# One transfer of weights at the end of a decode step comes as eight

## The chip, the cores and the metric

The kernel runs on one core of one Trainium2 chip. A core has a matrix engine (PE, with its weight loads shown apart as PEld), a vector engine (DVE), a scalar engine (ACT), a general engine (POOL) and SP, which here only issues transfers; 16 DMA engines move the data between the chip's memory (HBM) and the on-chip buffer of 128 partitions. The metric is the device time of one execution in microseconds (us). The kernel before took 527.71 us, the median of three runs from 527.6 to 528.53.

## The reference

Two equal layers work on one token of 640 numbers. Each is attention over a window of 4096 cached keys and values (32 heads of 192), and then a gated feed-forward network of 1536 columns, both with a layer norm in front and a residual sum behind. In short:

```
x = x + A(layernorm(x), k_cache, v_cache, wq, wo)
x = x + B(layernorm(x), w1, w3, w2)
x = x + A(layernorm(x), k_cache, v_cache, wq, wo)
x = x + B(layernorm(x), w1, w3, w2)

def B(x, w1, w3, w2):
    gate = x @ w1          # 640 -> 1536
    up = x @ w3            # 640 -> 1536
    h = silu(gate) * up
    return h @ w2          # 1536 -> 640
```

All weights and caches are bf16, and both layers use the same ones. With one token every weight is used once a layer, so the work is little beside the bytes: 221 MB are read.

## The kernel before

All large operands pass through one buffer, the arena, of 16 slots of 128 partitions by 6144 bf16 (12 KB a partition). A list, `loads`, written out ahead, holds every transfer in the order in which it is to be issued: for each layer wq, then keys and values head by head, then wo, then w1, w3 and w2. `refill()` takes entries from the front of that list as long as slots are free, and issues each of their parts as one transfer from SP (line 243). `done()` frees a slot when its last reader has been written out, and calls `refill()` again. SP does nothing else but issue these, and, at the very end, the transfer of the output (line 531). `pin()` keeps the order of the program on each engine.

The framework gives each transfer a completion semaphore; in the trace eight of them are handed out in turn (numbers 100, 102 and 105 to 110). A transfer's completion is marked by its DMA engines on that semaphore.

In layer 1 the feed-forward part has its weights in these entries: `("fa", 1)`, all of w1, 1920 KB in one transfer; `("fb", 1)`, the first four fifths of w3, 1536 KB; `("fc", 1)`, the rest of w3, 384 KB; and `("fd", 1)`, the first 5760 columns of w2 as it lies on the partitions (nine of its twelve chunks of 640 columns), in three transfers of 3840, 1280 and 640 columns, 960, 320 and 160 KB. The last three chunks of w2 stay in the tile `keep` since layer 0. The third transfer of `("fd", 1)` is the last load of the whole kernel.

`ffn(1)` multiplies by w1, turns the result and forms the gate, multiplies by w3, forms h in `htd`, and calls `last_rows`. That goes through the twelve chunks of w2 in the order 9, 10, 11 (from `keep`), 0 to 8 (from the arena); each is four small matmuls (tile `pss`, line 80, where the helper `mm` records all matmuls) that sum into one place. Chunks 0 to 5 lie in the first of the three transfers, 6 and 7 in the second, 8 in the third. Then DVE casts the sum (line 529) and SP sends it out (line 531). After that only the waits that close the program follow (line 603).

Where a matmul reads what several transfers have written, it stands behind all of them. All 128 partitions of a chunk are summed in one matmul, so a chunk is needed whole.

Of the kernel before, what the change touches and what calls it, by code (L numbers as in the profile page):

```python
# [15 lines left out]
P = 128  # L16
# [9 lines left out]
PGW = 6144  # L26
# [21 lines left out]
def kernel(  # L48
# [13 lines left out]
    nc = tc.nc  # L62
# [12 lines left out]
    def pin(ins):  # L75
        tc.keep_in_program_order(ins)
        return ins
# [61 lines left out]
    arena = arn.tile([P, NSLOT * PGW], BF16, name="arena")  # L139
# [6 lines left out]
    loads = []  # L146
# [5 lines left out]
    w2_v = B_w2.rearrange("(p f) n -> p (f n)", f=12)  # L152
# [3 lines left out]
    def slots(key, width):  # L156
        return [key] + [key + (i,) for i in range(1, -(-width // PGW))]

    def head(layer, g):
        return HG * ORDER[layer][g // HG] + g % HG  # L160

    def k_head(layer, g):
        return HG * ORDER[1][0] + (0, 3, 1, 2, 6, 4, 5, 7)[g] if layer == 1 and g < HG else head(layer, g)

    def k_first(layer, i):
        return layer == 0 and H - HB <= i < H
# [6 lines left out]
    def wo_units(layer):  # L173
        order = wo_order(layer)
        ends = (0, 8, 17, 26, 35, 44, 48) if layer == 0 else (0, 12, 24, 36, 44, 48)
        return [order[a:b] for a, b in zip(ends, ends[1:])]

    for layer in range(2):
        for c0, c1 in ((0, 1), (1, 2), (2, 3), (3, 5)) if layer == 0 else [(c, c + 1) for c in range(NCH)]:
            w = PGW // 2 if layer == 1 and c1 == NCH else PGW * (c1 - c0)  # L180
            loads.append(([("q", layer, c) for c in range(c0, c1)],
                          [(o, w, wq_r[:, PGW * c0 + o:PGW * c0 + o + w]) for o in range(0, PGW * (c1 - c0), w)]))
        for i in range(H + LEAD):
            kinds = (("v", i - LEAD, A_v_cache), ("k", i, A_k_cache))
            for kind, g, cache in kinds[::-1] if k_first(layer, i) else kinds:
                if not 0 <= g < H:
                    continue
                h = k_head(layer, g) if kind == "k" else head(layer, g)
                if kind == "k" and layer == 1 and h in RETAIN:
                    if h == STASH:  # L190
                        loads.append(([("k", 1, h)], []))
                    continue
                loads.append(([(kind, layer, h)],
                              [(0, PGW, cache[0, h, S0:SK, :].rearrange("(p t) d -> p (t d)", p=P))]))
        units = wo_units(layer)
        for w, unit in enumerate(units):
            parts = []
            for at, ci in enumerate(unit):
                blk, e = ORDER[layer][ci // 12], ci % 12
                if parts and parts[-1][2] == blk and parts[-1][3] + parts[-1][1] == e:  # L200
                    parts[-1][1] += 1
                else:
                    parts.append([at, 1, blk, e])
            if layer == 1 and w + 2 == len(units):
                (at, n, blk, e), = parts
                parts = [[at, n - 3, blk, e], [at + n - 3, 3, blk, e + n - 3]]
            parts = [(640 * at, 640 * n, wo_v[blk][:, 640 * e:640 * (e + n)]) for at, n, blk, e in parts]
            if w + 1 < len(units):
                loads.append((slots(("o", layer, w), 640 * len(unit)), parts))
            elif layer == 0:  # L210
                assert len(parts) == 1 and parts[0][1] == 2560
                loads.append((None, [(wo5[:], parts[0][2])]))
        rows = 4 if layer == 0 else 5
        loads.append((slots(("fa", layer), 1536 * rows), [(0, 1536 * rows, w1_v[:, 0:1536 * rows])]))
        loads.append(([("fb", layer)], [(0, PGW, w3_v[:, 0:PGW])]))
        if layer == 0:
            loads.append(([("fc", layer)], [(0, 1536, w1_v[:, PGW:]), (1536, 1536, w3_v[:, PGW:]),
                                            (3072, 2560, w2_v[:, 0:2560])]))
            loads.append(([("fd", layer)], [(0, 3200, w2_v[:, 2560:5760])]))
            loads.append((None, [(keep[:], w2_v[:, 5760:7680])]))  # L220
        else:
            loads.append(([("fc", layer)], [(0, 1536, w3_v[:, PGW:])]))
            loads.append(([("fd", layer)], [(o, n, w2_v[:, o:o + n]) for o, n in ((0, 3840), (3840, 1280), (5120, 640))]))

    def refill():
        while loads:
            keys, parts = loads[0]
            if keys is None:
                for dst, src in parts:
                    pin(nc.sync.dma_start(out=dst, in_=src))  # L230
                loads.pop(0)
                continue
            n = len(keys)
            at = [s for s in free if all(s + i in free for i in range(n))]
            if not at:
                return
            s = at[0]
            for i, key in enumerate(keys):
                free.remove(s + i)
                home[key] = s + i  # L240
            loads.pop(0)
            for off, w, src in parts:
                pin(nc.sync.dma_start(out=arena[:, s * PGW + off:s * PGW + off + w], in_=src))
            if not parts:
                stash(arena[:, s * PGW:s * PGW + PGW], False)

    def stash(x, save):
        xu, pu, ru = x.bitcast(U32), pss[:].bitcast(U32), rest[:].bitcast(U32)
        at = 0
        for t, lo, n in [(pu, 512 * k, 512) for k in range(5)] + [(pu, MB + MN, 512 - MN), (ru, 0, MN)]:  # L250
            a, p = xu[:, at:at + n], t[:, lo:lo + n]
            pin(nc.vector.tensor_copy(out=p if save else a, in_=a if save else p))
            at += n
# [4 lines left out]
    def done(*keys):  # L258
        for key in keys:
            free.append(home.pop(key))  # L260
        refill()
# [272 lines left out]
    def attention(layer):  # L534
# [36 lines left out]
        wo_proj(layer)  # L571

    refill()
    for layer in range(2):
        attention(layer)
# [32 lines left out]
```

## Time and profile before

| | us |
|---|---|
| median of three runs (527.6 to 528.53) | 527.71 |
| the profiled execution's own time | 527.9 |
| its span, first to last instruction | 526.2 |
| PE busy | 278.6 |
| DVE busy | 257.9 |
| ACT busy | 62.0 |
| POOL busy | 16.3 |
| last 160 KB of w2: issued at | 507.18 |
| its time from issue to landing | 15.7 |
| output transfer: issued at | 523.62 |

Times in the profile count from the first instruction. "Busy" is the time in which an engine ran instructions. A transfer's issue is the short instruction on SP that starts it; its landing is the moment when its last completion mark arrives. The granted TensorE clock was 0.697 of full speed in the mean over the span. Over the span 422 GB/s were moved.

### The profile page before, as it was taken

The page shows a single profiled execution, that of the slowest core. Times are in us where ns is not written, and L with a number is a line of the kernel's source. Part 1 is how long each engine was busy: PE and PEld are TensorE (multiplying, and loading weights), DVE is VectorE, ACT ScalarE, POOL GpSimd, SP SyncE. Part 2 cuts the span into 40 slices and gives each one's busy share as a digit, 9 for nine tenths or more (in the row PEclk, how much of TensorE's full clock was granted, in tenths as well). Part 3 has the DMA queues.
Part 4 walks back from the last instruction along what each step waited for, and adds up shares of the span by engine and source line. Part 5 has one row for each costly group of instructions (what it writes and reads, how often), then busy time and mean ns, then how long its engine had stood idle before and what let it go on. Part 6 is the DMA issues. An engine that isn't in the chain of part 4 may idle for free.

```text
span 526.2 us, 5967 instructions
## 1 busy us (share of the span) xinstructions
PE 278.6 (53%) x2403; PEld 114.8 (22%) x2403; DVE 257.9 (49%) x389; ACT 62.0 (12%) x192; POOL 16.3 (3%) x76
## 2 busy tenths in 40 slices
PE   3434654473655645645545566687254756355545
PEld 1111221131212211212112222233022322122122
DVE  1099875556757476653002137722476655753001
ACT  1001120110202020102001002022111120102000
POOL 4000000000000000000000000000000000001000
PEclk9657878667766776586556557988657886686558
DMA  8999999999999999999999999999999999999995
GB/s 345 432 430 429 428 428 432 430 430 429 428 430 427 428 432 431 426 430 420 418 429 424 424 429 427 430 427 431 426 430 428 430 426 432 429 429 428 433 425 240
DMA packets 21779, 221.80 MB, mean 422 GB/s; under 512 B 2552, under 2 KB 2680, under 8 KB 4856
## 3 DMA queue, kind: packets, MB, share of 16 engines
q1 hardware_dynamic: 21608, 221.42, 99.2%
q8 instruction: 19, 0.31, 0.2%
q14 instruction: 8, 0.07, 0.0%
q10 hardware_dynamic: 144, 0.00, 0.0%
HBM read 221.41 MB, written 0.00 MB: 421 GB/s over the span
## 4 chain that ended last, share of the span: by engine, by line
DMA 46%; PE 5%; DVE 4%; issue 1%; ACT 0%; SPq 0%; DVEq 0%; ACTq 0%
DMA arena<-in_A_v_cache_dram 24%; DMA arena<-in_A_wo_dram 9%; DMA arena<-in_A_k_cache_dram 7%; DMA arena<-in_B_w_dram 4%; DVE arena L330 3%; DMA arena<-in_A_wq_dram 2%; PE s_ps L80 1%; PE y_ps L80 1%; PE o_ps L80 1%; PE q_ps L80 1%; PE pss L80 1%; PE g_ps L80 0%; DVE w L278 0%; ACT w L364 0%; DVE lt L352 0%
## 5 line engine op out<-in xcount | busy, mean ns | idle before, releaser
L80 PE MATMUL s_ps<-arena,wst 128*32 128x512 bf16 x768 | 154.7, 519 | 167.1 <-DVE arena L330 84.1
L330 DVE STREAM_TRANSPOSE arena<-arena 128x1536 uint32<-128x1536 uint32 x100 | 171.1, 1754 | 61.8 <-DMA arena<-in_A_k_cache_dram 61.4
L80 PE MATMUL o_ps<-arena,ptm 128*8 128x384 bf16 (+1 forms) x1024 | 113.2, 422 | 17.6 <-DMA arena<-in_A_v_cache_dram 17.6
L80 PEld LDWEIGHTS <-wst 128*32 128x32 bf16 x768 | 53.7, 117 | 251.9 <-issue 224.5
L80 PEld LDWEIGHTS <-ptm 128*8 128x8 bf16 (+1 forms) x1030 | 40.1, 99 | 54.9 <-issue 43.6
L361 ACT ACTIVATE nt<-m 32x16 f32<-32x16 f32 x16 | 3.4, 213 | 271.5 <-DVE m L358 271.5
L377 ACT COPY ptm<-w 32x64 bf16<-32x64 bf16 x80 | 23.6, 295 | 47.8 <-PE o_ps L80 45.4
L80 PE MATMUL q_ps<-arena,xs 128*32 128x512 bf16 x120 | 17.8, 599 | 15.6 <-DMA arena<-in_A_wq_dram 13.0
L410 DVE SCALAR_TENSOR_TENSOR w<-pss,sc,cb 64x192 bf16<-64x192 f32 x16 | 6.7, 417 | 37.3 <-PE pss L80 34.2
L80 PE MATMUL y_ps<-arena,otd 128*1 128x320 bf16 x176 | 15.1, 461 | 14.3 <-DMA arena<-in_A_wo_dram 14.3
L312 POOL COPY wst<-qt_sb 32x24 bf16<-32x24 bf16 x30 | 8.4, 281 | 432.7 <-PE s_ps L80 311.9
L367 DVE STREAM_TRANSPOSE w<-w 64x512 bf16<-64x512 bf16 x16 | 11.3, 705 | 14.4 <-ACT w L364 14.4
L352 DVE TENSOR_REDUCE lt<-s_ps 64x1 f32<-64x512 f32 x16 | 11.0, 684 | 14.0 <-PE s_ps L80 13.7
L377 DVE COPY ptm<-w 32x64 bf16<-32x64 bf16 x48 | 9.9, 207 | 15.7 <-PE o_ps L80 14.7
L278 DVE CAST w<-y_ps 128x320 bf16<-128x320 f32 x3 | 1.5, 492 | 32.9 <-PE y_ps L80 32.9
L80 PEld LDWEIGHTS <-xs 128*32 128x32 bf16 x200 | 8.8, 117 | 33.9 <-issue 25.2
L297 DVE CAST w<-q_ps 128x256 bf16<-128x256 f32 x2 | 0.8, 424 | 31.1 <-ACT w L296 31.1
L382 DVE RECIPROCAL sc<-pss 64x1 f32<-64x1 f32 x16 | 2.6, 166 | 21.5 <-PE pss L80 21.4
L403 ACT CAST w<-o_ps 128x384 bf16<-128x384 f32 x16 | 7.7, 478 | 35.3 <-PE o_ps L80 26.3
L80 PEld LDWEIGHTS <-otd 128*1 128x1 bf16 x192 | 6.5, 107 | 23.7 <-issue 19.5
L364 ACT ACTIVATE w<-s_ps,nt 64x512 bf16<-64x512 f32 x16 | 10.9, 682 | 5.7 <-DVE nt L362 5.7
L80 PE MATMUL pss<-w,sel 128*64 128x192 bf16 x32 | 6.5, 293 | 7.9 <-ACT w L403 5.1
(78 smaller groups left out, 111.2 us busy)
## 6 DMA issues: line engine op xcount, KB each, us to landing
arena<-in_A_v_cache_dram SPq DMA_DIRECT2D x64, 1536.0 KB, 29.2
arena<-in_A_k_cache_dram SPq DMA_DIRECT2D x50, 1536.0 KB, 29.2
arena<-in_A_wq_dram SPq DMA_DIRECT2D x7, 1536.0 KB, 9.3
arena<-in_A_wo_dram SPq DMA_DIRECT2D x3, 1920.0 KB, 31.6
arena<-in_B_w_dram SPq DMA_DIRECT2D x3, 1536.0 KB, 11.5
arena<-in_A_wq_dram SPq DMA_DIRECT2D x1, 3072.0 KB, 19.5
arena<-in_A_wo_dram SPq DMA_DIRECT2D x2, 1440.0 KB, 8.6
arena<-in_A_wo_dram SPq DMA_DIRECT2D x2, 960.0 KB, 8.1
```

The lines of the kernel that those rows point to most:

```text
L80: return pin(nc.tensor.matmul(*a, **k))
L278: pin(nc.vector.tensor_copy(out=y_sb[:, 320:640], in_=y_ps[1][:, 0:320]))
L312: pin((engs[a].copy if engs[a] is nc.scalar else engs[a].tensor_copy)(out=dst, in_=src))
L330: pin(nc.vector.transpose(x[:, w * sp:w * (sp + 1)].bitcast(U32), x[:, w * sp:w * (sp + 1)].bitcast(U32)))
L352: pin(nc.vector.reduce_max(out=t0[:, 0:1], in_=s_ps[0:64, :], axis=AX.X))
L361: pin(nc.scalar.mul(out=tb[32:64, :].rearrange("p (a z) -> p a z", a=4)[:, :, 0:HB], in_=mb, mul=-SCALE))
L364: pin(nc.scalar.activation(out=e[:], in_=s_ps[0:64, :], func=ACTF.Exp, bias=nbt[:, 0:1], scale=SCALE, accum_out=l[0:64]))
L367: pin(nc.vector.transpose(et[:], e[:]))
L377: pin((eng.copy if eng is nc.scalar else eng.tensor_copy)(out=dst, in_=src))
L382: pin(nc.vector.reciprocal(out=rl[half], in_=rl_ps[half]))
L403: pin(nc.scalar.copy(out=o_sb[:, 0:384], in_=o_ps[:, 0:384]))
L410: pin(nc.vector.scalar_tensor_tensor(out=om, in0=ot_ps[half], scalar=rl[half], in1=mask[half].unsqueeze(2).broadcast_to([64, 16, 12]), op0 ...
```

## The change

The last transfer, chunk 8 of w2 for layer 1 (640 columns, 1280 bytes on each of 128 partitions), is replaced by eight transfers of the same columns that take 64, 14, 12, 10, 8, 6, 4 and 10 of the partitions, in this order. To this end a part in `loads` may carry a first partition and a number of partitions, and `refill()` uses them. What is computed, and all other transfers and their order, stay as they are.

```
-            loads.append(([("fd", layer)], [(o, n, w2_v[:, o:o + n]) for o, n in ((0, 3840), (3840, 1280), (5120, 640))]))
+            parts = [(o, n, w2_v[:, o:o + n]) for o, n in ((0, 3840), (3840, 1280))]
+            p0 = 0
+            for rows in (64, 14, 12, 10, 8, 6, 4, 10):
+                parts.append((5120, 640, w2_v[p0:p0 + rows, 5120:5760], p0, rows))
+                p0 += rows
+            assert p0 == P
+            loads.append(([("fd", layer)], parts))
...
-            for off, w, src in parts:
-                pin(nc.sync.dma_start(out=arena[:, s * PGW + off:s * PGW + off + w], in_=src))
+            for off, w, src, *rows in parts:
+                p0, n = rows or (0, P)
+                pin(nc.sync.dma_start(out=arena[p0:p0 + n, s * PGW + off:s * PGW + off + w], in_=src))
```

## The prediction

> **What bounds the kernel now.** I read the page's 40 slices first: the DMA row stands at 9 from the second slice to the last but one, so the loads set the pace and the arithmetic hides behind them. The change touches only the last 160 KB, so the rest is read from the chain that ended last, whose tail is:
>
> ```profile
> 474.66 32.51 DMA arena<-in_A_wo_dram
> 507.16 0.02 issue
> 507.18 15.71 DMA arena<-in_B_w_dram
> 522.90 0.04 issue
> 522.94 0.27 PE pss L80 x4
> ```
>
> Columns are start, length and what. The load that is to be cut up is issued at 507.18 and lands at 522.90; the four matmuls of the last chunk start 0.04 later, then one cast (0.32) and the output transfer. Every us by which the landing moves, the end moves. The chain also goes back from the issue at 507.18 to the landing of *another* load, 0.02 earlier. Counting the issues of SP, that load (474.66) is the eighth before it. So I looked at what SP waits for between 486 and 510 us:
>
> ```profile
> SPq L243 <- DMA arena<-in_A_wo_dram: 12.6, 3, 4.2
> SPq L243 <- DMA arena<-in_A_v_cache_dram: 10.5, 3, 4.0
> ```
>
> All six last issues of line 243 waited for a landing. The semaphores of the trace say which: loads take eight completion semaphores in turn, and each issue waits until the earlier load of its own semaphore has landed. Even the output transfer, next in SP's order, passes such a wait at 509.1, before it waits for its data:
>
> ```profile
> L531 SPq EVENT_SEMAPHORE  x1: 14502/14502/14502, 509.1 to 509.1; - x1
> ```
>
> So never more than eight loads are under way, and a load's issue time is the landing time of its eighth predecessor. From the page's issue rows (KB, median us from issue to landing) these landings follow:
>
> ```profile
> arena<-in_B_w_dram SPq DMA_DIRECT2D x1, 960.0 KB, 23.6
> ...
> arena<-in_B_w_dram SPq DMA_DIRECT2D x1, 320.0 KB, 19.9
> arena<-in_B_w_dram SPq DMA_DIRECT2D x1, 160.0 KB, 15.7
> ```
>
> The 960 KB load, issued at 498.10, lands at 521.7; the 320 KB one, issued at 502.63, at 522.5. The last view is the DMA share stage by stage (us; PE, PEld, DVE, ACT, POOL busy; clock; DMA share; GB/s):
>
> ```profile
> 518.00:519.00 1.00, 0.50 (x10) 0.35 (x14) 0.55 (x3) 0.00 (x0) 0.00 (x0) 0.84 1.02 419
> 519.00:520.00 1.00, 1.00 (x18) 0.39 (x8) 0.00 (x0) 0.00 (x0) 0.00 (x0) 1.00 0.77 314
> 520.00:521.00 1.00, 0.40 (x4) 0.00 (x0) 0.55 (x1) 0.00 (x0) 0.00 (x0) 1.00 0.57 224
> 521.00:522.00 1.00, 0.65 (x28) 0.57 (x31) 0.20 (x2) 0.00 (x0) 0.00 (x0) 1.00 0.23 90
> 522.00:523.00 1.00, 0.75 (x36) 0.43 (x24) 0.00 (x0) 0.00 (x0) 0.00 (x0) 1.00 0.14 41
> ```
>
> The engines run dry one after the other: the 16 completion marks of the last load come between 519.15 and 522.90. The slowest engine alone sets the landing.
>
> **The change part by part.** The removed transfer put 8 rows of 1280 B on each of 16 engines. On the slowest they cost 0.37 us (its mark for the 320 KB load is at 522.53, for this one at 522.90), 46 ns a row. The first new transfer, 64 rows, leaves 4 on each. If none of the seven small ones reaches the slowest engine it is done 4 x 46 = 0.18 us sooner, if all do, 3 rows or 0.14 us later. That is the whole effect on the data itself.
>
> The larger term is the issue. Eight transfers take eight semaphores, so each waits for a landing of its own. In their order these are, from issue plus time to landing and to the hundredth from the trace's semaphore marks: 507.16 (as now), 509.07 and 510.28 (two wo loads), 514.82 (the 1920 KB load of w1), 518.45 and 519.39 (w3), 521.74 (the 960 KB of w2) and 522.53 (the 320 KB). None of these moves, since the pieces stand behind them on every engine. SP needs 0.33 us for an issue, and the gaps are wider, so SP itself is no limit. The first six pieces are issued by 519.4 and are over before the end: even at the upper 2.49 us worked out below, the sixth lands at 521.9. The seventh, issued at 521.76, is always 0.8 us ahead of the eighth. The eighth, 10 rows, can't be issued before 522.55, when almost all data is in. Nobody covers what follows: the last chunk's matmuls need all 128 rows. Behind it on SP only the output transfer waits; its own semaphore is by then that of the first piece, done at about 522.7, so it adds no wait.
>
> How long does a lone small load take from issue to landing? No row before shows one on empty engines, so I bound it from the two ends of the trace, where the engines were idle:
>
> ```profile
> 1.20:1.70 0.50, 0.00 (x0) 0.00 (x0) 0.00 (x0) 0.50 (x1) 0.50 (x4) 1.00 0.00 0
> 1.70:1.80 0.10, 0.00 (x0) 0.00 (x0) 0.00 (x0) 0.10 (x1) 0.10 (x2) 1.00 3.59 614
> ...
> 523.50:524.80 1.30, 0.00 (x0) 0.00 (x0) 0.05 (x1) 0.00 (x0) 0.00 (x0) 1.00 0.00 0
> ```
>
> SP's first load is issued at 0.74 (0.39 us of issue) and its first packet starts at 1.75; the output transfer is issued at 523.62 (0.65 us) and its first packet starts at 524.87. Both come 0.60 to 0.62 us after the issue has ended. The output's four rows are marked as landed by 525.27, 1.65 us after its start. The very first 12 KB packets took 0.74 to 1.28 us where later ones took 0.46, so a first read costs 0.28 to 0.82 us more. A completion mark comes 0.10 us (deep queue) to 0.34 us (output) after its packet. The row takes 0.055. Lower end: 0.33 + 0.62 + 0.06 + 0.28 + 0.10 = 1.39 us. Upper end: 0.65 + 0.62 + 0.06 + 0.82 + 0.34 = 2.49 us. The nearest row is the output transfer, a few rows on idle engines: 1.65 + 0.28 for the read = 1.93 with its issue of 0.65, or 1.61 with the 0.33 of nearly all loads. Nothing tells the two apart, so I take the middle, 1.77.
>
> By the Trainium skill (DMA: Bandwidth & Descriptors, section on the anatomy of one DMA, given there for the GpSimd path) a transfer costs about 2.0 us whatever its size, most of it the confirmation of the write, and the page says to coalesce small transfers. With 2.0 in place of 1.77 the time would be 0.23 us longer, 529.5; the trace's 1.65 for the output lies a little under that figure.
>
> Before the last chunk's matmuls PE now waits for eight semaphores where it waited for one. A waiting instruction on PE takes 0.051 us (its rows on line 603). Those for early pieces pass beforehand; if the last piece's is asked first, up to seven follow: 0 to 0.36 us, and as SP's rows on line 603 pair two semaphores, I take two, 0.10.
>
> Sum: issue 522.55 + 1.77 = 524.32 against 522.90, +1.42, plus 0.10 gives +1.52 us. The profiled execution took 527.9 us (span 526.2), 0.19 above the median of 527.71. So 529.4 on its own scale, and 529.23, say 529.2, beside the median.
>
> **The rivals.** *No wait, a better balance.* If the eight transfers could all be queued by 520.9, so that a lone one would land by 522.7, the slowest engine would set the end with as few as 4 rows, and the end would come 0.18 us earlier: 527.5. For it: the marks spread over 3.75 us, so shifting rows off late engines is what the data needs. Against it: every one of the last issues waits on its own semaphore's landing. 10%. By the Trainium skill (same page, section on why a DMA increments its semaphore by 16) a transfer uses the largest number of engines up to 16 that divides its rows, the lowest-numbered ones; engines 14 and 15 would then keep 4 rows and engines 0 to 3 get 11. The output's 4 rows agree: 12 marks at once at 524.64, four more at 525.21 to 525.27. Which engines are late the trace doesn't say.
>
> *Pieces that wait for each other.* If pieces with the same columns counted as overlapping, each would wait for the one before to land: first landing about 522.7, seven more at 1.77 + 0.05 each, 535.4, 12.5 us later, or 540.3. Against it: copies into the same columns of ptm, other rows, run abreast on two engines:
>
> ```profile
> 243.41 1.54 ACT L377 COPY ptm<-w 32x64 bf16<-32x64 bf16 x5 [2.44 <-PE o_ps L80]
> 243.42 0.42 DVE L377 COPY ptm<-w 32x64 bf16<-32x64 bf16 x2 [1.71 <-PE o_ps L80]
> ```
>
> 4%.
>
> **How the numbers follow.** About 0.2%, 1.06 us, is what a measurement of this kernel can tell from no change. The forecast, a last piece issued at 522.55, has 85%; 1% is left for what I don't see. Its own ends: 1.39 - 0.35 + 0 = +1.04 and 2.49 - 0.35 + 0.36 = +2.50, so 528.75 to 530.2; the median itself moves by 0.1 to 0.2 between runs, which makes the range 528.5 to 530.3. It leaves out the two rivals and a little of the forecast's edges. Of the 85%, 5% ends under +1.06. Faster 0.01, same 0.10 + 0.05 = 0.15, slower 0.84 (forecast 0.80, waiting pieces 0.04).
>
> **What would show it.** In the profile after: seven more issues on SP, at about 509.1, 510.3, 514.8, 518.5, 519.4, 521.8 and 522.55; the last piece 1.4 to 2.5 us from issue to landing; the chain's end passing from the 320 KB load through SP to a short load; a DMA share near zero for about a us before the last matmuls; four matmuls 0.04 to 0.4 us behind that landing, and all after that as now. I am wrong if the eighth piece is issued before 520.9, if a lone load lands in under 1.4 us, or if issues stand 1.8 us apart.

## The result and the profile after

The changed kernel takes 529.59 us (median of eight runs), the kernel before, on the same chips, 527.91. The ratio is 1.0034 with a 95% interval of 1.0023 to 1.0044, so 1.2 to 2.3 us slower. Forecast were 529.2 us and +1.5 us. The profiled span went from 526.2 to 527.7 us; a second profile of the kernel before, taken later, has 526.0.

The end of the chain that ended last, after (start, length, what):

```profile
502.28 20.36 DMA arena<-in_B_w_dram
522.63 0.02 issue
522.65 1.41 DMA arena<-in_B_w_dram
524.06 0.35 issue
524.41 0.27 PE pss L80 x4
524.68 0.02 issue
524.70 0.32 DVE w L536
```

Where before one load ran from 507.18 to the end, the chain now goes from the 320 KB load, landed at 522.63, through SP to a piece of 10 rows that is issued 0.02 us later and takes 1.41 us. Then there are 0.35 us, which were 0.04 before, until the four matmuls. From their start to the end of the span it takes 3.3 us, as before.

SP's issues in order of time (start, length), one view for each:

```profile
506.83 0.58 SPq L250 DMA_DIRECT2D arena<-in_B_w_dram  x1
...
514.55 0.28 SPq L250 DMA_DIRECT2D arena<-in_B_w_dram  x1
518.20 0.27 SPq L250 DMA_DIRECT2D arena<-in_B_w_dram  x1
519.11 0.27 SPq L250 DMA_DIRECT2D arena<-in_B_w_dram  x1
521.87 0.25 SPq L250 DMA_DIRECT2D arena<-in_B_w_dram  x1
522.65 0.28 SPq L250 DMA_DIRECT2D arena<-in_B_w_dram  x1
```

Two more stand at 508.74 and 509.94. These are the eight forecast times within 0.4 us. The DMA share by stage around the last issue (us; PE, PEld, DVE, ACT, POOL; clock; DMA share; GB/s) shows the empty time that follows it:

```profile
522.80:523.20 0.40, 0.19 (x8) 0.00 (x0) 0.00 (x0) 0.00 (x0) 0.00 (x0) 1.00 0.01 3
523.20:523.50 0.30, 0.00 (x0) 0.00 (x0) 0.00 (x0) 0.00 (x0) 0.00 (x0) 1.00 0.00 0
523.50:523.80 0.30, 0.00 (x0) 0.00 (x0) 0.00 (x0) 0.00 (x0) 0.00 (x0) 1.00 0.14 43
```

The ten rows of the last piece move between 523.5 and 523.7; no other load moves data from 523.0 on.

One thing in the trace was not forecast. These are the latest completion marks of each load after the change, worked out from the trace's semaphore marks, with the number of rows:

```
320 KB load                      522.63
64 rows  (piece 1)               522.84
14 rows  (piece 2)               523.03
12 rows  (piece 3)               523.24
10 rows  (piece 4)               523.43
 8 rows  (piece 5)               523.63
 6 rows  (piece 6)               523.84
 4 rows  (piece 7)               523.26
10 rows  (piece 8)               524.06
```

Pieces 2 to 6 were issued by 519.1, yet their last marks come 0.19 to 0.21 us apart, one row each, where a row was worth 46 ns. A slow engine that takes part in all six of them would be done at 523.84 even if nothing had been issued late. So there were two theories for the experiments. **L** (late issue): the eighth piece waits for the 320 KB load, then needs 1.41 us, then PE 0.35. **M** (marks): every piece in which an engine takes part costs it about 0.2 us.

### The profile page after: what moved, and what is told of

It reads as the page before. It is cut to its first block, busy times and chain, and to the rows that moved or that the text cites. A ratio compares the mean times of both kernels' runs of the same rounds, so it can differ in the third digit from the quotient of the medians.

```text
span 527.7 us, 5977 instructions
## 1 busy us (share of the span) xinstructions
PE 287.6 (55%) x2403; PEld 117.7 (22%) x2403; DVE 257.9 (49%) x389; ACT 62.1 (12%) x192; POOL 16.3 (3%) x76
## 4 chain that ended last, share of the span: by engine, by line
DMA 45%; PE 6%; DVE 4%; ACT 1%; issue 1%; SPq 0%; DVEq 0%; ACTq 0%
DMA arena<-in_A_k_cache_dram 19%; DMA arena<-in_A_v_cache_dram 9%; DMA arena<-in_A_wo_dram 9%; DMA arena<-in_B_w_dram 4%; DVE arena L337 3%; PE s_ps L80 2%; DMA keep<-in_B_w_dram 2%; DMA arena<-in_A_wq_dram 2%; PE o_ps L80 1%; PE y_ps L80 1%; PE q_ps L80 1%; PE pss L80 1%; ACT w L371 0%; DVE lt L359 0%; PE g_ps L80 0%
## 5 line engine op out<-in xcount | busy, mean ns | idle before, releaser
L80 PE MATMUL s_ps<-arena,wst 128*32 128x512 bf16 x768 | 160.5, 537 | 158.6 <-DVE arena L337 79.3
L80 PE MATMUL o_ps<-arena,ptm 128*8 128x384 bf16 (+1 forms) x1024 | 115.0, 429 | 18.8 <-DMA arena<-in_A_v_cache_dram 18.8
L80 PEld LDWEIGHTS <-wst 128*32 128x32 bf16 x768 | 54.9, 120 | 246.9 <-issue 221.9
L80 PE MATMUL q_ps<-arena,xs 128*32 128x512 bf16 x120 | 18.9, 623 | 16.6 <-DMA arena<-in_A_wq_dram 14.0
```

The source lines that it names most:

```text
L80: return pin(nc.tensor.matmul(*a, **k))
```

## The experiments

Apart from the waits of PE taken early, the pieces ahead of the 320 KB load, the kernel before once more and the halves by columns, every edit is to the list of rows alone, which is `(64, 14, 12, 10, 8, 6, 4, 10)` in the changed kernel. "X" below is the latest mark of the 320 KB load in the same profile; before, the last landing was X + 0.37.

**Five pieces, all issued early**

```
-            for rows in (64, 14, 12, 10, 8, 6, 4, 10):
+            for rows in (64, 16, 16, 16, 16):
```

> Two theories of the 1.5 us. Theory L (late issue): the last piece is issued only when the 320 KB load has landed and then needs 1.41 us, and PE needs 0.35 us for eight waits. Theory M (marks): in the trace after, the marks of the first six pieces on the slowest DMA engine come 0.20 us apart (522.84, 523.03, 523.24, 523.43, 523.63, 523.84) although a row costs it 0.05, so every piece that an engine takes part in costs it about 0.2 us, however few its rows. This kernel has five pieces of 64, 16, 16, 16 and 16 rows: the same bytes on every engine as one transfer, and the last piece is issued when the 1536 KB load of w3 has landed (about 518.2), far ahead of the end. L: the last landing is as before, 0.4 us behind the last mark of the 320 KB load, and only one or two more waits on PE cost 0.1 to 0.2: 0.1 to 0.2 us slower than before. M: the slowest engine ends its 64-row share 0.21 us behind its last mark of the 320 KB load and then needs 4 x 0.2, so landing 1.0 us behind that mark: 0.7 to 0.9 us slower than before.

Measured: 1.0027 (1.0017 to 1.0038), 0.9 to 2.0 us slower. The chain's end and two stages of the DMA share:

```profile
518.11 5.38 DMA arena<-in_B_w_dram
523.49 0.09 issue
523.58 0.27 PE pss L80 x4
```

```profile
522.00:522.40 0.40, 0.34 (x20) 0.18 (x9) 0.00 (x0) 0.00 (x0) 0.00 (x0) 1.00 0.09 29
522.40:522.80 0.40, 0.25 (x8) 0.10 (x7) 0.00 (x0) 0.00 (x0) 0.00 (x0) 1.00 0.00 0
```

The last piece is issued at 518.11 and lands at 523.49, X + 0.98 (X is 522.51), as M said (1.0). The latest marks of the five pieces stand at 522.68, 522.89, 523.09, 523.29 and 523.49. All data has moved by 522.4, as the second view shows: no packet after that (the last ends at 522.38). So it isn't the rows that take 0.2 us each but the completion marks, the last of which trails the last row by 1.1 us. Without any late issue, pieces of one row for each engine make the kernel slower. The time lies above the 0.7 to 0.9 us that M gave; about 0.2 us of it comes after the output has landed, as the run with four quarters shows below.

**Eight pieces, six of them on two engines alone**

```
+            for rows in (96, 2, 2, 2, 2, 2, 2, 20):
```

> Eight pieces of 96, 2, 2, 2, 2, 2, 2 and 20 rows. If a two-row piece goes to two engines alone, the slowest engine (which took part in the six-row piece of the kernel after, but not in its four-row piece) has the first and the last piece only: two marks. The last piece is still issued when the 320 KB load has landed. L: as the kernel after, landing 1.4 us behind that load, PE 0.35 us: about 1.5 us slower than before. M alone: landing 0.5 to 0.6 us behind the 320 KB load's last mark (0.3 for six rows, 0.2 for one more piece), with PE's waits 0.3 to 0.5 us slower than before.

Measured: 1.0045 (1.003 to 1.006). The chain:

```profile
522.58 1.52 DMA arena<-in_B_w_dram
524.11 0.35 issue
524.46 0.33 PE pss L80 x4
```

The 96 rows are complete at X + 0.19 and none of the six small pieces has a mark behind 523.12, so M has nothing to say here, and still the end comes at X + 1.54: issue at 522.58, 1.52 us for the load, 0.35 for PE. L alone is enough as well, though 1.6 to 3.2 us are a little more than the 1.5 it gave.

**The waits of PE taken early**

```
         for fcx in (9, 10, 11, 0, 1, 2, 3, 4, 5, 6, 7, 8):
             pg, off = w2_chunk(1, fcx)
+            if fcx == 8:
+                mm(pss[0:1, 512:513], lhsT=htd[0:118, 8:9], rhs=pg[0:118, off:off + 1], start=True, stop=True)
```

> The kernel after with one more matmul of one column ahead of the last chunk, into an unused place, that reads rows 0 to 117 of the chunk, so that it waits for the first seven pieces; only the last piece's wait is left for the last chunk. If PE's 0.35 us between the last landing and the matmuls are the eight waits in a row, this falls to 0.05 to 0.1 and the time is 0.25 to 0.3 us under the kernel after (1.2 to 1.3 us slower than before). If the 0.35 us are something else (PE gone cold, the landing seen late), it stays at 0.35 and the time is that of the kernel after. The landing itself stays 1.4 us behind the 320 KB load.

Measured: 1.0029 (1.0018 to 1.004), span 527.4 against 527.7. The chain:

```profile
521.83 1.53 DMA arena<-in_B_w_dram
523.36 0.51 issue
523.87 0.16 PE pss L80
524.03 0.03 issue
524.06 0.27 PE pss L80 x4
```

The load in the first line is piece 7, with 4 rows. The last piece lands at 524.02 and the four matmuls start at 524.06: 0.35 us became 0.04, and 0.51 us of waits now stand ahead of the extra matmul, beside the last piece's way. In the time alone the gain can't be told, as the interval overlaps that of the changed kernel (1.0023 to 1.0044). In the changed kernel these waits are three instructions in PE's queue, the first of which asks for the last piece's semaphore together with that of piece 7; the others, though long satisfied, follow it at 0.1 us each. The view names the group without the semaphores, which stand in the trace:

```profile
L80 PEldq EVENT_SEMAPHORE  x3: 51/51/51, 524.1 to 524.3; - x3
```

**Seven pieces, the last issued 0.76 us earlier**

```
+            for rows in (64, 14, 12, 10, 8, 6, 14):
```

> Seven pieces of 64, 14, 12, 10, 8, 6 and 14 rows: the last is issued when the 960 KB load has landed (0.76 us earlier than in the kernel after). L alone: it lands 1.4 us after that, 0.65 us behind the last mark of the 320 KB load, PE 0.25 to 0.35: 0.5 to 0.7 us slower than before. M: the slowest engine, in all seven pieces, still ends at 0.21 + 6 x 0.2 = 1.41 us behind that mark, so as the kernel after, 1.4 to 1.6 us slower than before: the two causes end together in the kernel after and taking one away gives nothing.

Measured: 1.0036 (1.0023 to 1.0049), as the changed kernel: nothing that can be measured was won by issuing earlier. In its profile the slowest engine's marks go 522.69, 522.89, 523.08, 523.28, 523.48, 523.68 and 523.89, which is X + 1.40, where M put it, although the last piece was issued at 521.75. One further row landed only at 525.26 in that execution: a 16 KB instruction fetch occupied a DMA engine from 522.7 for 1.5 us, and a row's packet starts as it ends (that both ran on one engine is read from these times alone). That mishap is part of neither theory; the profiled execution took 530.88 us, where the median of its kernel is 529.07.

**Two halves and four quarters by rows**

```
+            for rows in (64, 64):
```

> Two pieces of 64 rows, both issued far ahead of the end. In the run with five pieces the marks of one engine came 0.17 to 0.20 us apart although all rows had been moved 1.1 us before the last mark, so the theory M is now: two marks of one engine are never under 0.17 to 0.20 us apart. Four rows take 0.18 us by themselves, so each of the two marks comes when its data allows it: landing 0.37 to 0.42 us behind the last mark of the 320 KB load, as before, and one more wait on PE: within 0.1 us of before. If a piece had a fixed cost on top of its rows instead (0.15 us and 0.05 a row), two pieces would land 0.7 us behind that mark: 0.3 to 0.4 us slower than before.

```
+            for rows in (32, 32, 32, 32):
```

> Four pieces of 32 rows, two rows on every engine in each, the last one issued when the 1920 KB load has landed, far ahead of the end. M: four marks 0.20 apart, landing 0.8 us behind the last mark of the 320 KB load instead of 0.37: 0.4 to 0.5 us slower than before, with PE's waits up to 0.6. Rows alone (46 ns each): landing as before, 0 to 0.2 us slower through PE's waits. A fixed cost on top of the rows: 4 x (0.15 + 0.1) = 1.0 us, 0.6 to 0.8 us slower.

Measured: two halves 1.0013 (1.0004 to 1.0022), four quarters 1.0019 (1.001 to 1.0028). The chains, first of the halves, then of the quarters:

```profile
522.77 0.04 issue
522.82 0.31 PE pss L80 x8
523.12 0.04 issue
523.16 0.27 PE pss L80 x4
```

```profile
514.77 8.71 DMA arena<-in_B_w_dram
523.48 0.04 issue
523.52 0.27 PE pss L80 x4
```

The halves land at X + 0.35 (marks 0.18 and 0.17 apart) and the quarters at X + 0.62 (0.16, 0.15, 0.15, 0.16). So a mark has no cost on top of its rows; two marks of one engine simply came no closer than 0.15 to 0.2 us in these profiles. That gives M its form: four rows hide it, two rows do so in part, one row doesn't. But the landings, -0.02 and +0.25 us against X + 0.37, don't explain the ratios, 0.7 and 1.0 us in the middle. X itself is later, 522.77 and 522.86. And the end of the program is longer: from the output's landing to the last instruction it takes 0.93 us before, 1.01 with the halves and 1.16 with the quarters and with the five pieces. There SP passes the waits of line 603 (610 in these kernels), two semaphores at a time and 0.06 us each. The number of loads decides which of the eight semaphores the output gets, and so how many of these waits still stand behind its own.

**The five pieces ahead of the 320 KB load**

```
-            parts = [(o, n, w2_v[:, o:o + n]) for o, n in ((0, 3840), (3840, 1280))]
+            parts = [(o, n, w2_v[:, o:o + n]) for o, n in ((0, 3840),)]
...
-            for rows in (64, 14, 12, 10, 8, 6, 4, 10):
+            for rows in (64, 16, 16, 16, 16):
...
+            parts.append((3840, 1280, w2_v[:, 3840:5120]))
...
-        for fcx in (9, 10, 11, 0, 1, 2, 3, 4, 5, 6, 7, 8):
+        for fcx in (9, 10, 11, 0, 1, 2, 3, 4, 5, 8, 6, 7):
```

> The five pieces of 64, 16, 16, 16 and 16 rows are issued ahead of the 320 KB load instead of behind it, and chunks 6 and 7 are multiplied last. If the marks only queue while the data goes on (M as it stands now), their 4 x 0.2 us run beside the 0.8 us of the 320 KB load's rows: its last mark comes as late as the last mark of all came before, and the time is within 0.2 us of before. If an engine's data stands still while it gives its marks, the pieces cost the same 0.6 us of landing as behind the load: 0.7 to 1.3 us slower than before, as with the five pieces behind it.

Measured: 1.0015 (1.0006 to 1.0024), 0.3 to 1.3 us slower. From the last mark of the 960 KB load to the last of all it is 1.21 us, against 1.16 before: the five marks ran beside the data of the 320 KB load, and the data wasn't held by the marks. In the landings the theory's point holds. In the time its bound of 0.2 us was missed: the middle, 0.8 us, is what was expected if data stood still. Part of that is a last mark of the 960 KB load that is late here, too (522.09, before 521.74); as long as that delay isn't explained, the time doesn't decide.

**Rows moved to four engines**

```
+            for rows in (60, 68):
```

> Two pieces of 60 and 68 rows, to see what moving rows off an engine is worth without late issue and with two marks. If the 60 rows go to 15 engines, four rows each, and the 68 to four engines, 17 rows each, the slowest engine has 4 rows or none in place of 8, unless it is one of those four. Then the landing comes 0.15 to 0.2 us behind the last mark of the 320 KB load instead of 0.37 and the time is about 0.2 us under before, less than a measurement here can tell; if the slowest is one of the four, it has 21 rows: 1.0 us behind that mark, 0.6 us slower than before.

Measured: 1.0006 (0.9997 to 1.0014), no difference. The latest mark of the 60 rows is at X + 0.17; the 68 rows give twelve marks at once and four more at 520.18, 520.87, 521.20 and 522.47. So they went to four engines, none of which was the last to finish, and the last landing came 0.2 us sooner relative to the 320 KB load. That is the effect of moving rows, and it is too small to be seen in the time. By the Trainium skill (DMA: Bandwidth & Descriptors, section on why a DMA increments its semaphore by 16) a transfer uses the largest number of engines up to 16 that divides its rows, and the others' marks are written at once; 68 rows on four engines and 60 on fifteen (one mark at once) agree.

Which engine is late isn't a fixed thing, though. In the changed kernel the slowest took part in the piece of 6 rows but not in that of 4. In the run with PE's waits taken early, with the same rows, the slowest took part in the piece of 14 (its mark 522.87) and not in that of 12, whose latest mark is 522.46. A split by engine number, chosen beforehand, would have missed the slow engine in one of the two.

**The kernel before once more**

No edit.

> The kernel before, unchanged, for a second profile. In the profiles with two and four pieces the last mark of the 320 KB load stands at 522.77 and 522.86 us, where the first profile of the kernel before has it at 522.53, and no step of the change reaches that load. If such a load's last mark scatters by some tenths between executions, it comes anywhere from 522.4 to 522.9 here; if the pieces behind it delay it, it stays at 522.5. The last mark of all comes 0.35 to 0.40 us behind it in either case.

Measured in its profile: X is 522.35, the last landing 522.72, again X + 0.37; the span is 526.0. So X scatters by 0.2 us between two executions of one kernel, but the other way than was needed. The two profiles agree on something better: the last mark of the 960 KB load comes 2.35 us behind that of the 384 KB load in both, and all 128 packets of it take exactly 291 ns. In each of the nine profiles with pieces by rows the distance is 2.53 to 2.78 us, in the changed kernel 2.76, and some packets take longer, up to 481 ns with the two halves. None of the long packets starts before the first row of the first piece has begun to move.

In the changed kernel the long packets are the smaller part of the delay, though. The last packet of the 960 KB load ends 2.34 us behind the last of the 384 KB load, against 2.30 before, and the last of the 320 KB load ends at 522.04, against 522.20 before. What comes late is mostly the marks: the last one of the 960 KB load stands 0.77 us behind its last packet (0.33 before), that of the 320 KB load 0.60 us (0.33 before). With the two halves the data itself is late as well (2.62 us between those last packets).

**Two halves by columns**

```
-            loads.append(([("fd", layer)], [(o, n, w2_v[:, o:o + n]) for o, n in ((0, 3840), (3840, 1280), (5120, 640))]))
+            loads.append(([("fd", layer)], [(o, n, w2_v[:, o:o + n]) for o, n in ((0, 3840), (3840, 1280), (5120, 320), (5440, 320))]))
```

> Two transfers again, but each of all 128 rows and half the columns, where the two-piece kernel took 64 rows and all columns. In both profiles of the kernel before the last mark of the 960 KB load comes 2.35 us behind that of the 384 KB load before it and every packet of it takes 291 ns; in all profiles with row pieces it is 2.5 to 2.8 us and some packets take up to 360 to 480 ns, so row pieces seem to hold up a load that was issued ahead of them. If that is because a piece of fewer rows has engines write to other partitions than their own load at that moment, beside the engine that is late there, then with column halves it is 2.35 us and 291 ns again, and the time is that of before within 0.1 us. If it comes from the number of transfers alone, it is 2.5 to 2.8 us again and the time 0.2 to 0.6 us over before, as with two row halves (ratio 1.0013).

Measured: 1.0003 (0.9994 to 1.0012), no difference, while two halves by rows cost 1.0013. The chain:

```profile
502.40 19.90 DMA arena<-in_B_w_dram
522.29 0.04 issue
522.34 0.67 PE pss L80 x12
```

The last mark of the 960 KB load is 2.34 us behind that of the one before it, every packet of it takes 291 ns, and the last landing is X + 0.42. So in the profiles it is not the number of transfers, but that they take part of the partitions, which goes with the loads ahead being complete 0.2 to 0.4 us later: nine profiles with row pieces and three without stand on either side of that gap. The times alone don't separate the two kinds of halves, as their intervals (1.0004 to 1.0022 and 0.9994 to 1.0012) overlap. Why is only argued: the Trainium skill (same page, section on the descriptor swizzle) says that in a transfer of 128 partitions each engine writes through a port of its own; a piece of 64 rows changes which engine writes which partition, so an engine that is early would write through the port of one that is late. The longer packets agree with that; no run here shows a port, and why the marks come late behind data that is on time stays open.

## Why the prediction was right, point by point

The direction and the late issue behind it were right: the eighth piece can't be issued before the 320 KB load has landed, and nothing covers its way. That the size fits so closely (+1.5 against 1.2 to 2.3 measured) is partly luck, as three terms were off and cancelled.

| term, relative to before | forecast | measured, changed kernel |
|---|---|---|
| last mark of the 320 KB load | 0 | 522.63 - 522.53 = +0.10 |
| last landing behind that mark | 1.79 - 0.37 = +1.42 | 1.43 - 0.37 = +1.06 |
| PE's waits | 0.14 - 0.04 = +0.10 | 0.35 - 0.04 = +0.31 |
| sum, the start of the last matmuls | +1.52 | 524.41 - 522.94 = +1.47 |

Against the second profile of the kernel before, the first row would be +0.28 (522.35) and the sum +1.65.

The prediction also had only one of the two causes in the transfers. The marks of the six early pieces end 0.22 us ahead of the late piece, and the runs with five and with seven pieces show that they alone make the kernel slower: without the late issue it would have been about as slow.

*The waits on the eight semaphores.* Right: the eighth piece is issued 0.02 us behind the landing of the 320 KB load.

*A lone load takes 1.77 us.* Mis-sized. It took 1.41, 1.52 and, in the run with PE's waits early, 1.44 us, near the lower end of 1.39; the first of these is just above the 1.4 below which the prediction would have called itself wrong. The surcharge for a first read (0.28 us) was hardly there: most of the ten packets took 53 ns. Its issue took 0.28 us, where the sum took the middle between 0.33 and 0.65. One entry of the lower end was misread: in the kernel before a completion mark comes 0.28 us behind the end of its last row (522.62, 522.90), not 0.10; for the lone load it is 0.36. The 2.0 us of the Trainium skill (DMA: Bandwidth & Descriptors, section on the anatomy of one DMA), given there for the GpSimd path, are above all three.

*PE's waits cost 0.10 us.* Mis-sized: 0.31, near the upper end. The bad case named there is what happened, the last piece's semaphore asked first, and each of the three waits steps on by 0.1 us, not by 0.051.

*"None of these moves, since the pieces stand behind them on every engine."* Wrong. The last mark of the 960 KB load moved from 2.35 to 2.76 us behind that of the 384 KB load. On the clock of the profile less of it is left, as the 384 KB load was 0.29 us earlier (519.10, before 519.39): the 960 KB load is complete at 521.86, before at 521.74 and 521.55, and the 320 KB load is later by the 0.10 to 0.28 us above.

*"That is the whole effect on the data itself" (-0.18 to +0.14).* Wrong for pieces that give an engine one or two rows: marks 0.15 to 0.2 us apart make the six early pieces end 0.84 us later than X + 0.37 on the slowest engine. For the same reason the sixth piece, put at 521.9 by the time of a lone load, landed at 523.84: it wasn't alone, but stood behind other loads and their marks. In the changed kernel this ends at 523.84, 0.22 us ahead of the late piece, so it was hidden, and the sum didn't need it. For the rows alone the term is right: 0.2 us with 60 and 68 rows.

*The rivals.* The first, a better balance if nothing had to wait, falls: five pieces without any late issue were 0.9 to 2.0 us slower, not 0.18 faster. Only the run with 60 and 68 rows came near its price: the last landing was 0.20 us closer to the 320 KB load, which the time (1.0006) doesn't show. The second, pieces that wait for each other, didn't occur: each was issued on its own load's landing, and no piece waited for another.

What stays open is why the marks of earlier loads come later beside row pieces, and how much of the first row of the table is scatter between executions.

## What to carry to other kernels

Before cutting a last transfer into pieces, count the completion semaphores: with eight in turn, the eighth piece can't be issued before the load ahead of the first has landed, and a lone load at the very end costs 1.4 to 1.5 us that nothing covers. No cut won anything here. If there must be one, cut by columns rather than by rows (two halves by columns cost nothing that could be measured, two by rows 0.2 to 1.2 us), and leave each engine several rows a piece: on one engine, completions came no closer than 0.15 to 0.2 us, with one row or two. And where one instruction must wait for several loads, let an earlier one take the waits for those that come early.

## What was not expected of the hardware

Completion marks are a resource of their own: on one engine they came 0.15 to 0.2 us apart while 1280-byte rows pass in 55 ns, and at the end of five pieces the last one trailed the last data by 1.1 us. In the one run with the small pieces ahead of a large load they ran beside its data (1.21 us from the 960 KB load's last mark to the end, against 1.16).

Beside transfers over part of the partitions, loads that had been issued earlier were complete later, with some packets of up to 481 ns where all others take 291. In the changed kernel it was mostly the marks that came late (0.77 and 0.60 us behind the last packets, 0.33 before), with two halves mostly the data. Two halves by columns showed neither.

At the end of a stream of 221 MB the slowest engine was 3.75 us behind the fastest (519.15 and 522.90 before), and by the pieces it took part in it wasn't the same engine in every profile.
